# Reordering the first steps and the last steps of a top-k attention and highway kernel, and warming TensorE from the start

## The chip, the cores and the metric

The kernel runs on one core of a Trainium2 chip. The metric is the device time of the whole program in microseconds (us), taken as the median of several runs; lower is better. A profile of one execution goes with it. Its span, from the first to the last instruction, is a little shorter than the time of the same run.

Engine names as the profile writes them: PE is TensorE (matmuls; PEld is its weight load), DVE is VectorE, ACT is ScalarE, POOL is GpSimd, SP is SyncE, which here only issues transfers.

## The reference

Two things are computed, one after the other: attention in which every query keeps only its 32 largest scores, and a highway layer on the joined heads.

```python
# q, k, v: (8 batches, 8 heads, 576 rows, 64), float32
scores = (q @ k.T) / sqrt(64)
kth    = 32nd largest of each row
attn   = softmax(where(scores >= kth, scores, -1e9))
x      = (attn @ v), heads joined            # (4608, 512)
H = maximum(x @ w_h, 0)
T = 1 / (1 + exp(-(x @ w_t + b_t)))
out = T * H + (1 - T) * x                    # (4608, 512)
```

## The kernel before

The work is cut into 144 pairs. A pair is 128 query rows of two heads (or, for the 64 rows left over in each batch, of four heads at half height), and 18 pairs make a batch. The main loop is a pipeline over steps: step `n` evacuates and searches pair `n` while it multiplies pair `n + 1`, transposes pair `n - 4` and multiplies the values of pair `n - 5`. Two pairs, that is four rows of scores in each partition, are searched together as one quad. The names of the tiles are the ones in the profile:

- `kin`, `qin`, `krest`, `qrest`, `qc`: inputs as loaded. PE transposes them into a PSUM tile `kqps`, and a copy brings them to `kq`.
- `ps`: raw scores in PSUM (one buffer of four banks). ACT copies them with a ReLU to `z`.
- `hi`, `hh`, `h`: the row of 576 folded to 288, 144 and 72 by pairwise maxima on DVE. POOL makes the minima of the folds in the same tiles.
- `m`, `w`: lists of the largest values, from MAX8 and MATCH_REPLACE8 on DVE. Their end is the threshold.
- `pen`: ACT's penalty for what lies below the threshold. PE transposes `z` and adds the scaled penalty in PSUM (`zr`, `zt`), ACT takes the exponential into `et`, and PE multiplies it by the values `v` into `zr`, from which ACT copies `xs`.
- `x`, `xT`, `hps`, `tps`, `t`, `d`, `o`: the highway layer of one group of rows, in three parts "x" (transpose `x`), "h" and "t" (the two matmuls).

The opening and the loop, cut to what matters:

```python
def turn(self, pr, name, hp, bank=None, c0=0):       # transpose inputs on PE
    pool, tag = (self.ztps, "zt") if bank else (self.fps, "fp")
    ...
    nc.scalar.copy(dst, kqps[:, c0 * P : J * P])

def spin(n):
    for _ in range(n):
        ops.nc.tensor.transpose(warm[:, 0:P], ident[:], ident[:])

spin(12)
ops.turn(pr, "kin", 0, True)
ops.turn_first(pr, 0, 1)
ops.turn_rest(pr, 0, 1, ("krest",))
# ... loads
ops.scores(0, *pairs[0], preps[0])
ops.evac(0)
ops.turn_first(pr, 1, NHP)
ops.turn(pr, "kin", 1, True)
ops.turn_rest(pr, 1, NHP, ("krest",))

while step <= NPR:
    n = step
    if have(n):
        ops.tree(n)                                  # DVE: hi <- max of halves
        if n % 2:
            ops.minima(n // 2, ops.folds(n // 2, *pairs[n - 1], fill))
        if n + 2 < NHP:
            ops.turn(pr, "kin", n + 2, True)
        ...
    # ... masks of pair n - 4, values of pair n - 5
    if have(n + 1):
        ops.scores(n + 1, g, pi, preps[g.b])         # PE, needs ps free
        ops.evac(n + 1)                              # ACT: z <- relu(ps)
    # ... "x" and "h" of the highway layer
    if kind == "t":
        ops.ffn_t(fg)                                # PE tps, ACT t, t
    if n % 2:
        # ... rest of the lists of the quad before
        if n == 1:
            opening = ops.lists(0, *pairs[0])
            ops.run(opening, 2)                      # 4 MAX8, 4 MATCH_REPLACE8
    else:
        gens = opening if n == 2 else ops.lists(n - 2, *pairs[n - 2])
        # ...
    if nextg:
        ops.ffn_x(nextg)                             # joint group: PE xtps, ACT xT
    if have(n - 4):
        ops.trans(n - 4)                             # PE zr, zt; ACT et
    ...
```

`nextg` occurs four times: every second batch the two halves of 64 left-over rows form a joint group, which ends right behind another group. Its transposes take one of the two `zt` buffers that the transposes of `z` use as well.

`tree(n)` reads `ps` itself for `n >= 2`, so that the scores of pair `n + 1` can't be multiplied before `tree(n)` is done on DVE; for the first two pairs it reads `z` only.

The end of the program finishes the last two groups `gp` and `gl`, in whose order DVE, ACT and PE work as written:

```python
ops.ffn_e(gp)
ops.ffn_o(gp, *out_rows(gp))        # POOL: o <- d - x, then a transfer
...
ops.final_norm(gl, 3, 4)            # DVE: x of the last two heads
...                                 # PE transposes it, DVE: xT, PE: hps, t
judge_last(gl)                      # DVE: are the lists good enough?
ops.ffn_d(gl)
ops.final_t(gl, 3, 4)
judge()                             # PE: turn 128 verdicts, DVE: flag
ops.final_o(gl, out_rows(gl), (nc.sync, ops.nc.scalar))   # DVE: d, o, d, o; transfers
...
taken = nc.values_load(flag[0:1, 0:1], min_val=0, max_val=1)
with tc.If(taken > 0):              # an exact second pass, not taken here
```

Of the kernel before, what the change touches and what calls it, by code (L numbers as in the profile page):

```python
# [11 lines left out]
FP32 = mybir.dt.float32  # L12
# [7 lines left out]
J = 4  # L20
NZ = 3
NPEN = 3


class Pinned:
# [42 lines left out]
class Ops:  # L68
# [103 lines left out]
    def turn(self, pr, name, hp, bank=None, c0=0):  # L172


        nc, P = self.nc, self.P
        t = pr.pop((name, hp))
        pool, tag = (self.ztps, "zt") if bank else (self.fps, "fp")
        kqps = pool.tile([P, 512], FP32, tag=tag, name="kqps")
        for c in range(c0, J):
            nc.tensor.transpose(  # L180
                kqps[:, c * P : (c + 1) * P],
                t[:, c, :, :].rearrange("p h d -> p (h d)"),
                self.ident[:],
            )
        dst = pr["kq"][:, "kq".index(name[0]), hp, c0 * P : J * P]
        nc.scalar.copy(dst, kqps[:, c0 * P : J * P])

    def turn_rest(self, pr, h0, h1, names=("krest", "qrest")):

# [444 lines left out]
            if i1 == n_g:  # L634
                nc.scalar.activation(tp, tp, AF.Tanh)

    def final_o(self, g, dsts, queues):


        vec, P = self.nc.vector, self.P  # L640
        W = self.dm // 2
        n = P // len(dsts)
        o = self.fpool.tile([P, self.dm], FP32, tag="o", name="o")
        for j, tp in enumerate(g.tp):
            cs = slice(j * W, (j + 1) * W)
            vec.scalar_tensor_tensor(
                out=g.d[:, cs], in0=tp, scalar=1.0, in1=g.d[:, cs],
                op0=ALU.add, op1=ALU.mult,
            )
            vec.tensor_tensor(o[:, cs], g.d[:, cs], g.x[:, cs], ALU.subtract)  # L650
            for i, dst in enumerate(dsts):
                queues[j].dma_start(dst[:, cs], o[i * n : (i + 1) * n, cs])

    def ffn_bank(self, g, name, other=False):
        if g.last:
# [102 lines left out]
    def ffn_o(self, g, *dsts):  # L758
        ql = g.rows
        n = ql // len(dsts)  # L760
        if not self.exact and not g.last:
            for i, dst in enumerate(dsts):
                self.nc.gpsimd.dma_start(
                    dst, g.t[i * n : (i + 1) * n, :], accum_op=ALU.add
                )
            return
        o = self.fpool.tile([self.P, self.dm], FP32, tag="o", name="o")
        self.nc.gpsimd.tensor_tensor(
            o[0:ql, :], g.d[0:ql, :], g.x[0:ql, :], ALU.subtract
        )  # L770
        for i, dst in enumerate(dsts):
            self.nc.sync.dma_start(dst, o[i * n : (i + 1) * n, :])
# [3 lines left out]
def kernel(  # L776
# [25 lines left out]
    def const(shape, dt, name):  # L802
        return consts.tile(shape, dt, tag=name, name=name)

    ident = const([P, P], FP32, "ident")
    make_identity(nc, ident[:])
    nident = const([P, P], BF16, "nident")
# [34 lines left out]
    with ExitStack() as cm:  # L842
# [53 lines left out]
                ops.load_values(pr)  # L896

        for b in range(1, B):
            f = first[b] - 17
            for hp in range(NHP):  # L900
                at(f + 3 * hp, begin, b, hp)
                for i, name in enumerate(("kin", "qin")):
                    at(
                        f + 3 + 3 * hp + i,
                        lambda b, name, hp: ops.turn(preps[b], name, hp),
                        b, name, hp,
                    )
            at(f + 5, lambda b: ops.turn_rest(preps[b], 0, NHP), b)
            at(f + 8, lambda b: ops.values_rest(preps[b]), b)
            at(f + 11, lambda b: ops.values(preps[b], 0), b)  # L910
            at(f + 14, lambda b: ops.values(preps[b], 1), b)
# [11 lines left out]
        ops.load_first(pr, queue, 2, H)  # L923
        ops.load_rest(pr, "krest", queue, 2, H)
        ops.load(pr, "kin", 2, queue)
        warm = ops.fps.tile([P, 512], FP32, tag="fp", name="warm")

        def spin(n):
            for _ in range(n):
                ops.nc.tensor.transpose(warm[:, 0:P], ident[:], ident[:])  # L930

        spin(12)
        ops.turn(pr, "kin", 0, True)
        ops.turn_first(pr, 0, 1)
        ops.turn_rest(pr, 0, 1, ("krest",))
# [6 lines left out]
        ops.evac(0)  # L942
        ops.turn_first(pr, 1, NHP)
        ops.load_rest(pr, "qrest", queue, tag="qc")
        ops.turn(pr, "kin", 1, True)
        ops.turn_rest(pr, 1, NHP, ("krest",))
        ffn = []
        step = 0
# [32 lines left out]
# [3 lines that stand above are left out]
                ops.tree(n)  # L984
                if n % 2:
                    ops.minima(n // 2, ops.folds(n // 2, *pairs[n - 1], fill))
                    fill = []
                if n + 2 < NHP:
                    ops.turn(pr, "kin", n + 2, True)
                if NHP <= n + 1 < 2 * NHP:  # L990
                    ops.turn(pr, "qin", n + 1 - NHP, None, 1)
                if n == NHP:
                    ops.load(pr, "qin", 3, None, None, 1)
                if n == 2 * NHP:
                    ops.turn_rest(pr, 0, NHP, ("qrest",))
            if n == 5:
                load_weights()
            if have(n - 4):
                ops.mask(n - 4, *pairs[n - 4], tis=(0,))
            kind = fg = None  # L1000
            nextg = None
            if ffn and (ffn[0][0] != "x" or n % 2):
                kind, fg = ffn.pop(0)
                if kind == "t" and ffn and ffn[0][0] == "x":
                    nextg = ffn.pop(0)[1]
            if have(n - 5):
                values(n - 5)
            if have(n - 4):
                ops.mask(n - 4, *pairs[n - 4], tis=(1,))
            if have(n + 1):  # L1010
                g, pi = pairs[n + 1]
                ops.scores(n + 1, g, pi, preps[g.b])
                ops.evac(n + 1)
            if kind == "x":
                ops.ffn_x(fg)
            if kind == "h":
                ops.ffn_h(fg)
                ops.ffn_r(fg)
                ops.ffn_d(fg)
            if kind == "t":  # L1020
                ops.ffn_t(fg)
                if n < NPR - 1:
                    ops.ffn_e(fg)
                    ops.ffn_o(fg, *out_rows(fg))
            if n == 3:
                ops.values_rest(pr)
                ops.values(pr, 0)
            if n == 4:
                ops.values(pr, 1)
            ended = False  # L1030
            if have(n - 5):
                g, pi = pairs[n - 5]
                ended = pi == len(g.pairs) - 1 and (not g.rem or g.r0 > 0)
            if n % 2:
                gens = ops.lists_rest(n // 2 - 1, *pairs[n - 3]) if have(n - 3) else []
                late = gens[2:]
                gens = gens[0:2]
                if n == 1:
                    opening = ops.lists(0, *pairs[0])
                    ops.run(opening, 2)  # L1040
                ops.run(gens)
                ops.run(late, 2)
            else:
                ops.run(late)
                if n == 2:
                    gens = opening
                else:
                    gens = ops.lists(n - 2, *pairs[n - 2]) if have(n - 2) else []
                    ops.run(gens, 2)
                if ended:  # L1050
                    ops.norm(pairs[n - 5][0])
                ops.run(gens, 3)
                if have(n + 1):
                    gens, fill = gens[0:2], gens[2:4]
                ops.run(gens)
            if nextg:
                ops.ffn_x(nextg)
            if have(n - 4):
                ops.trans(n - 4)
            if ended and not pairs[n - 5][0].last:  # L1060
                ops.norm_heads(pairs[n - 5][0])
            for piece in pieces.pop(n, []):
                piece()
            if n % 2 == 0 and have(n - 3):
                g, pi = pairs[n - 3]
                if pi == len(g.pairs) - 1:
                    ops.settle(g)
            if ended:
                g = pairs[n - 5][0]
                ffn += [("x", g), ("h", g), ("t", g)]  # L1070
            step += 1
# [20 lines left out]
        ops.run(gens)  # L1092
        ops.mask(m + 1, *pairs[m + 1])
        ops.ffn_h(gp)
        ops.run(late)
        ops.settle(gl)
        ops.mask(m + 2, *pairs[m + 2])
# [1 line left out]
        ops.final_norm(gl, 0, 2)  # L1099
        ops.trans(m + 1)  # L1100
        ops.ffn_r(gp)
        ops.ffn_d(gp, ops.ffn_t(gp))
        judge_lists()
        judge_scales()
        part, ends = ops.parts(
# [12 lines left out]
        gl.ps = ops.fps.tile([P, 512], FP32, tag="fp", name="hps")  # L1118
        ops.final_norm(gl, 2, 3)
        ops.ffn_e(gp)  # L1120
        ops.ffn_o(gp, *out_rows(gp))
        values(m + 2)
        ops.final_h(gl, 0, 2)
        ops.final_turn(
            gl, 2, 3, ops.ztps.tile([P, 512], FP32, tag="zt", name="xtps")
        )
        ops.final_norm(gl, 3, 4)
        ops.final_t(gl, 0, 2)
        ops.final_turn(
            gl, 3, 4, ops.ztps.tile([P, 512], FP32, tag="zt", name="xtps")  # L1130
# [4 lines left out]
        ops.final_h(gl, 3, 4)  # L1135
        ops.ffn_d(gl)
        ops.final_t(gl, 3, 4)
        judge()
        ops.final_o(gl, out_rows(gl), (nc.sync, ops.nc.scalar))

    taken = nc.values_load(flag[0:1, 0:1], min_val=0, max_val=1)
    with tc.If(taken > 0):
# [72 lines left out]
```

## Time and profile before

| | |
|---|---|
| time, median of 3 runs | 838.0 us (837.43 to 838.75) |
| the profiled run | 837.23 us, span 835.4 us |
| DVE busy | 813.4 us, 97% of the span |
| ACT busy | 760.8 us, 91% |
| PE busy | 698.5 us, 84% |
| POOL busy | 711.5 us, 85% |
| share of DVE in the chain of work that ended last | 83% |
| transfers | 58.12 MB, 70 GB/s in the mean |

Busy time is the time in which an engine executes something; the rest of the span it waits. The chain of work that ended last is followed back from the last instruction: at each step either the instruction before it on the same engine, or, where the engine had been waiting, the one that released it. The timeline lists instructions in order of time: start, duration, engine, line, operation, result and operands, shapes, how many of them, and in square brackets how long the engine had been idle and what ended that. Nearly all operations carry line 35, a recording helper, so that they are told apart by their tiles. The clock of TensorE is given as the share of full speed that was granted; it is known from 7.4 us of the span on, and shown as 1.00 before that.

### The profile page before, as it was taken

The numbers are of one execution on the slowest core, as the hardware profiler recorded it, in microseconds if no ns is written. First come the engines' busy times: TensorE is split into PE (matmuls) and PEld (weight loads), VectorE is DVE, ScalarE is ACT, GpSimd is POOL, SyncE is SP. The second block draws the span as 40 slices with busy tenths as digits, with TensorE's granted clock in tenths as the row PEclk, the third lists the DMA queues.
The fourth block names the chain that finished last, engine by engine and source line by source line (L and its number), as shares of the span: only waits on it lengthen the run. The fifth ranks groups of instructions, "written<-read, shape, count | busy, mean of one in ns | idle before, by whom it ended". The sixth has DMA issues, their size and how long they took to land.

```text
span 835.4 us, 20051 instructions
## 1 busy us (share of the span) xinstructions
PE 698.5 (84%) x6520; PEld 488.4 (58%) x6566; DVE 813.4 (97%) x4169; ACT 760.8 (91%) x1522; POOL 711.5 (85%) x457
## 2 busy tenths in 40 slices
PE   6688888888888888788888898878888888878875
PEld 4466556565566556665556565656556665556554
DVE  4999999999999999999999999999999999999896
ACT  4799999899999999899999999989999999888894
POOL 6788888898889889878889988888888989887882
PEclk9999999999999999999999999999999999999898
DMA  8563523234254431333325242323413211111221
GB/s 191 135 110 71 115 39 67 57 69 96 39 100 86 78 89 32 72 70 66 88 52 98 64 112 41 64 58 67 111 40 67 50 31 34 40 39 27 38 39 43
DMA packets 105184, 58.12 MB, mean 70 GB/s; under 512 B 82288, under 2 KB 91888, under 8 KB 105072
## 3 DMA queue, kind: packets, MB, share of 16 engines
q1 hardware_dynamic: 93200, 37.47, 17.6%
q0 software_dynamic: 11056, 19.01, 15.6%
q8 instruction: 53, 0.87, 0.4%
q14 instruction: 59, 0.48, 0.2%
q10 hardware_dynamic: 816, 0.30, 0.1%
HBM read 30.67 MB, written 18.35 MB: 59 GB/s over the span
## 4 chain that ended last, share of the span: by engine, by line
DVE 83%; ACT 8%; PE 7%; issue 1%; POOL 1%; DVEq 0%; ACTq 0%; POOLq 0%
DVE w L35 46%; DVE m L35 18%; DVE hi L35 10%; DVE hh L35 5%; DVE h L35 3%; ACT pen L35 2%; PE zt L35 2%; PE ps L35 2%; ACT z L35 1%; ACT x L35 1%; ACT et L35 1%; ACT t L35 1%; PE hps L35 1%; PE zr L35 1%; DVE scales L35 0%
## 5 line engine op out<-in xcount | busy, mean ns | idle before, releaser
L35 PE MATMUL ps<-kq 64*128 64x64 f32 (+3 forms) x1280 | 206.7, 446 | 50.4 <-DVE hi L35 47.2
L35 ACT ACTIVATE pen<-z,m 128x576 bf16<-128x576 f32 x288 | 226.6, 788 | 1.1 <-DVE m L35 0.9
L35 PE MATMUL zt<-ident,z 128*128 128x128 f32 x1148 | 215.4, 281 | 6.1 <-ACT xT L35 6.1
L35 PE MATMUL zt<-nident,pen 128*128 128x128 bf16 x1148 | 205.9, 220 | 0.0
L35 ACT ACTIVATE z<-ps 128x1152 f32<-128x1152 f32 x144 | 162.8, 1131 | 46.8 <-PE ps L35 44.3
L35 POOL TENSOR_TENSOR hi<-z,hi 128x1152 int32<-128x1152 int32 x72 | 189.3, 2630 | 12.4 <-DVE m L35 6.9
L35 POOL TENSOR_TENSOR hi<-hi,z 128x1152 int32<-128x1152 int32 x72 | 190.3, 2643 | 5.6
L35 PEld LDWEIGHTS ps<-kq 64*128 64x128 f32 (+1 forms) x1280 | 104.9, 180 | 145.4 <-issue 81.7
L35 PEld LDWEIGHTS zt<-ident,z 128*128 128x128 f32 x1148 | 163.1, 142 | 21.3 <-ACT xT L35 7.0
L35 ACT ACTIVATE et<-zt 128x512 bf16<-128x512 f32 x287 | 162.5, 601 | 7.6 <-PE zt L35 3.8
L35 POOL TENSOR_TENSOR hh<-hi,hh 128x576 int32<-128x576 int32 x71 | 103.3, 1455 | 71.7 <-DVE w L35 71.7
L35 PEld LDWEIGHTS <-pen 128*128 128x128 bf16 x1440 | 152.4, 106 | 16.1 <-ACT pen L35 10.7
L35 DVE MAX8 m<-w 128x8 f32<-128x168 f32 x576 | 159.2, 316 | 0.0
L35 PE MATMUL zr<-v,et 128*128 128x65 bf16 (+1 forms) x1590 | 98.5, 196 | 46.1 <-ACT et L35 38.6
L35 PEld LDWEIGHTS <-et 128*128 128x128 bf16 (+1 forms) x1600 | 69.3, 101 | 84.4 <-ACT et L35 82.1
L35 DVE MAX8 w<-hi 128x8 f32<-128x288 f32 x288 | 115.8, 441 | 0.1
L35 DVE TENSOR_TENSOR hi<-ps,z 128x576 f32<-128x576 f32 x142 | 104.7, 738 | 4.3 <-ACT z L35 3.9
L35 POOL TENSOR_TENSOR hh<-hh,hi 128x576 int32<-128x576 int32 x71 | 100.3, 1412 | 5.6
L35 DVE MAX8 w<-hh 128x8 f32<-128x72 f32 x576 | 96.8, 219 | 0.0
L35 DVE MATCH_REPLACE8 w<-m,w 128x168 f32<-128x168 f32 x288 | 88.8, 314 | 0.0
L35 PE MATMUL zr<-ident,z 128*128 128x128 f32 x286 | 68.9, 294 | 9.2 <-ACT xs L35 9.2
L35 ACT ACTIVATE x<-xs,scales 128x64 f32<-128x64 f32 x272 | 68.2, 336 | 0.0
(96 smaller groups left out, 1152.3 us busy)
## 6 DMA issues: line engine op xcount, KB each, us to landing
x<-d POOLq DMA_DIRECT2D x34, 256.0 KB, 3.9
vin<-in_v_dram SPq DMA_DIRECT2D x8, 1024.0 KB, 5.5
kin<-in_k_dram SPq DMA_DIRECT2D x63, 128.0 KB, 3.3
out_dram<-d SPq DMA_DIRECT2D x30, 256.0 KB, 2.2
out_dram<-t POOLq DMA_DIRECT2D x30, 256.0 KB, 4.1
qin<-in_q_dram SPq DMA_DIRECT2D x56, 128.0 KB, 2.9
qrest<-in_q_dram SPq DMA_DIRECT2D x8, 128.0 KB, 3.8
vrest<-in_v_dram SPq DMA_DIRECT2D x8, 128.0 KB, 2.8
```

What stands on the lines that cost most here:

```text
L35: return self._tc.keep_in_program_order(fn(*args, **kw))
```

## The change

It moves work, and adds a little, in five places:

1. The first quad is searched whole in step 2: its first eight list operations no longer stand ahead of `tree(2)` on DVE.
2. TensorE is kept at work from the start. A tile of zeros, which DVE fills first of all, takes the place of the identity that POOL builds; 8 matmuls of 512 columns on it stand in front of the first transposes, and 9, 7 and 8 more behind the scores of steps 1, 2 and 3. They write to a PSUM tile that nobody reads.
3. In the opening, the copy of the transposed second `kin` goes to DVE, and the transposes of the third and fourth stand behind the scores of their step and not ahead of them. The loads and transposes for the second batch begin two steps later.
4. The transposes of a joint group's `x`, and with them ACT's copy `xT`, stand ahead of the "t" matmuls of the group before it, and no longer behind them and the lists.
5. At the end, the "t" matmuls of `gp` stand earlier, its last subtraction is done by DVE in place of POOL and stands behind the norm of the last heads, and the verdict and its flag are made behind the last output and not ahead of it.

```diff
+WARM = {1: 9, 2: 7, 3: 8}
...
     def turn(...):
-        nc.scalar.copy(dst, kqps[:, c0 * P : J * P])
+        copy = nc.vector.tensor_copy if bank == "V" else nc.scalar.copy
+        copy(dst, kqps[:, c0 * P : J * P])
...
     def final_o(self, g, dsts, queues, finish):
...
                 queues[j].dma_start(dst[:, cs], o[i * n : (i + 1) * n, cs])
+        finish()
...
     def ffn_o(...):
-        self.nc.gpsimd.tensor_tensor(
+        (self.nc.gpsimd if self.exact else self.nc.vector).tensor_tensor(
             o[0:ql, :], g.d[0:ql, :], g.x[0:ql, :], ALU.subtract
...
+    idle = const([P, 512], BF16, "idle")
+    nc.vector.memset(idle[:], 0.0)
...
-            f = first[b] - 17
+            f = first[b] - (17 if b > 1 else 15)
...
-        warm = ops.fps.tile([P, 512], FP32, tag="fp", name="warm")
         def spin(n):
+            if n:
+                warm = ops.ztps.tile([P, 512], FP32, tag="zt", name="warm")
             for _ in range(n):
-                ops.nc.tensor.transpose(warm[:, 0:P], ident[:], ident[:])
-        spin(12)
+                ops.nc.tensor.matmul(
+                    warm[:], idle[:, 0:P], idle[:], start=True, stop=True
+                )
+        spin(8)
...
-        ops.turn(pr, "kin", 1, True)
+        ops.turn(pr, "kin", 1, "V")
...
-                if n + 2 < NHP:
-                    ops.turn(pr, "kin", n + 2, True)
...
                 ops.scores(n + 1, g, pi, preps[g.b])
                 ops.evac(n + 1)
+                if n + 2 < NHP:
+                    ops.turn(pr, "kin", n + 2, True)
+            spin(WARM.get(n, 0))
             if kind == "x":
...
+            if nextg:
+                ops.ffn_x(nextg)
             if kind == "t":
                 ops.ffn_t(fg)
...
-                if n == 1:
-                    opening = ops.lists(0, *pairs[0])
-                    ops.run(opening, 2)
...
-                if n == 2:
-                    gens = opening
-                else:
-                    gens = ops.lists(n - 2, *pairs[n - 2]) if have(n - 2) else []
-                    ops.run(gens, 2)
+                gens = ops.lists(n - 2, *pairs[n - 2]) if have(n - 2) else []
+                ops.run(gens, 2)
...
-            if nextg:
-                ops.ffn_x(nextg)
...
         ops.ffn_h(gp)
+        h = ops.ffn_t(gp)
...
-        ops.ffn_d(gp, ops.ffn_t(gp))
+        ops.ffn_d(gp, h)
...
-        ops.ffn_o(gp, *out_rows(gp))
...
         ops.final_norm(gl, 3, 4)
+        ops.ffn_o(gp, *out_rows(gp))
...
-        judge()
-        ops.final_o(gl, out_rows(gl), (nc.sync, ops.nc.scalar))
+        ops.final_o(gl, out_rows(gl), (nc.sync, ops.nc.scalar), judge)
```

## The prediction

> **What bounds the kernel now.** I read the page's busy shares and its chain of work first: DVE is busy 813.4 of 835.4 us, and 83% of the chain that ended last is DVE.
>
> ```profile
> PE 698.5 (84%) x6520; PEld 488.4 (58%) x6566; DVE 813.4 (97%) x4169; ACT 760.8 (91%) x1522; POOL 711.5 (85%) x457
> ...
> DVE 83%; ACT 8%; PE 7%; issue 1%; POOL 1%; DVEq 0%; ACTq 0%; POOLq 0%
> ```
>
> So whatever the change does, it can only win time in which DVE waits: 835.4 - 813.4 = 22.0 us, or work that it takes from DVE (none; it adds three instructions). The next view is therefore the waits of DVE alone, and then the timeline around each.
>
> ```profile
> DVE kq L35 <- PE kqps L35: 8.2, 2, 5.6
> DVE hi L35 <- ACT z L35: 6.3, 4, 2.3
> DVE xT L35 <- PE xtps L35: 0.8, 2, 0.5
> DVE w L35 <- POOL room L35: 0.4, 1, 0.4
> ```
>
> They lie in three places. The opening: no work but two copies before 9.19 us, then a wait to 12.29 and one to 21.11, 12.2 us in all. The joint groups: 0.1 us each at 243, 443 and 644, and 2.5 us behind the fourth. The end: about 1.4 us of small waits, and 4.9 us from DVE's last result to the end. Between 22 and 226 us, and in all the long stretches between, DVE does not wait; nothing can be won there.
>
> The timeline of DVE in the opening, of PE there, of PE, ACT and DVE behind the fourth joint group, and of DVE and POOL at the end:
>
> ```profile
> 12.29 0.76 DVE L35 TENSOR_TENSOR hi<-z 128x576 f32<-128x576 f32 x1 [2.34 <-ACT z L35]
> ...
> 18.77 0.90 DVE L35 MAX8 w<-hh 128x8 f32<-128x72 f32 x6
> 21.11 0.76 DVE L35 TENSOR_TENSOR hi<-ps,z 128x576 f32<-128x576 f32 x1 [1.45 <-ACT z L35]
> ```
>
> ```profile
> 17.56 2.35 PE L35 MATMUL ps<-kq 64*128 64x512 f32 x8 [3.96 <-DVE hi L35]
> ...
> 22.02 1.30 PE L35 MATMUL ps<-kq 64*128 64x512 f32 x8 [1.28 <-DVE w L35]
> ```
>
> ```profile
> 774.74 0.33 PE L35 MATMUL zt<-ident,z 128*128 128x128 f32 x1 [1.73 <-ACT xT L35]
> ...
> 776.82 2.40 PE L35 MATMUL ps<-kq 64*128 64x512 f32 x8
> ```
>
> ```profile
> 779.26 1.13 ACT L35 ACTIVATE z<-ps 128x1152 f32<-128x1152 f32 x1 [1.40 <-PE ps L35]
> ```
>
> ```profile
> 780.42 0.76 DVE L35 TENSOR_TENSOR hi<-ps,z 128x576 f32<-128x576 f32 x1 [1.99 <-ACT z L35]
> ```
>
> ```profile
> 824.01 0.29 DVE L35 TENSOR_TENSOR x<-xs,scales 128x128 f32<-128x128 f32 x1
> ...
> 825.01 1.39 DVE L35 TENSOR_TENSOR x<-xs,scales 128x128 f32<-128x128 f32 x1
> ...
> 828.72 0.14 DVE L35 CAST flag<-flag_f 1x1 int32<-1x1 f32 x1
> ...
> 830.02 0.42 DVE L35 TENSOR_TENSOR o<-d,x 128x256 f32<-128x256 f32 x1
> ```
>
> ```profile
> 824.98 1.26 POOL L35 TENSOR_TENSOR o<-d,x 128x512 f32<-128x512 f32 x1 [4.34 <-DVE scales L35]
> ```
>
> To be seen: the same eight score matmuls take 1.30 us at full clock and 2.35 to 2.40 after TensorE had stood still; behind the fourth joint group the chain is ACT xT, PE zt, PE ps at half clock, ACT z, DVE hi; and at the end one and the same DVE operation takes 0.29 us, and 1.39 where POOL's o runs beside it.
>
> [...]
>
> **The change, part by part.**
>
> *First chain.* The first kin has landed at 4.09 us (from the transfers' landing times), and the 12 warm transposes hold PE until 4.19, so its transposes start at 4.22. The new tile of zeros is a short DVE fill that I put at 0.7 to 1.0 us, so warming starts about 0.5 us before today's 1.58. But eight 512-column matmuls at half clock take about 0.43 us each (the four "t" matmuls of the trace take 1.03 us at full clock, 0.21 each once they are pipelined), 3.4 us, and hold PE until about 4.45: the chain starts 0.2 us later. In return the clock rises, in the mean, 0.5 us earlier, which is worth half of that. [...]
>
> *Copies of the opening.* [...] The third kin is out of PE's way, so scores(1) start at 9.7 in place of 9.78. But its copy now stands behind z(1), from 12.1 to 12.65, and scores(2) need it: 12.7 in place of 12.30. They are done at 14.0, z(2) at 15.2, and DVE wants it at 15.4. It just fits: 0.1 us.
>
> *First quad.* tree(2) moves from 16.75 to 15.4, as the 4 MAX8 and 4 MATCH_REPLACE8 (15.40 to 16.75) now follow it. ps is free at 16.16. The 9 warm matmuls, 9 x 0.215 = 1.9 us, begin at 14.55 and end near 16.5; scores(3) run at full clock from 16.5 to 17.8, z(3) to 18.9. DVE's list work from tree(2) to tree(3) is 1.35 + 1.33 + 0.90 = 3.6 us less overlaps, so it comes to tree(3) at 19.65 and doesn't wait. Gain 21.11 - 19.65 = 1.46. Part of it is given back: POOL's two minima of the first quad (15.64 to 20.95) do not move, since they start when the folds end, and the two-input fold hh behind tree(3) now meets them (20.45 against 20.87), so it is held 0.4 us. Net 1.05 us. The later start of the second batch's loads takes work from a stretch in which DVE doesn't wait: 0.
>
> *Joint groups.* xT comes behind z and ahead of two activations of 0.58 and 0.63 us, so it ends 1.15 us earlier (773.54 for 774.69), and PE waits 0.5 us and not 1.73. ACT loses its gap of 0.33 us, comes to the next z at 777.5, and the scores, if the clock holds, end at 777.8. DVE gets z at 779.0 where it was ready at 778.44: it waits 0.56 in place of 1.99, and the later 0.50 and 0.11 go as well: 2.0 us. The other three give up 0.1 each. [...] I take 1.8 us.
>
> *End.* o costs DVE about 0.69 us (512 of 576 columns of a 0.76 us operation), but frees x of its lock: x ends at 825.30 for 826.39, o at 825.95, xT at 826.24 for 827.17. The d, o, d, o behind it then end at 829.2 for 830.45, also because flag and cast (0.41) stand behind them: 1.3 us sooner for the last transfer. But the flag is made at 829.55 for 828.86, 0.7 us later, and each engine loads it and branches on it. Before, SP branches at 830.2, 1.35 us after the flag because a transfer was in its way, and its first event behind the branch comes at 833.14, 0.03 us after the transfer issued by SP landed (833.11). So either landing (then the end gains 1.3) or the time behind the branch, 2.9 us on SP and 3.1 on DVE, sets the end; with the branch at flag + 1.0 = 830.55 the end would lose 0.3. I take +0.1.
>
> Sum: 0 + 0 + 1.05 + 1.8 + 0.1 = 3.0 us, so 838.0 - 3.0 = 835.0 us.
>
> **Rivals.** [...] (b) *The end gains in full*, because landing and not the branch sets it: 833.8. (c) *The joint groups give nothing*, as another wait takes the place of xT: ACT is at 91% and in these steps has no slack, so that z comes late whatever PE does: 836.8. Against it: ACT does wait for PE there, 0.33 and 1.40 us. (d) *DVE's new work at the front or at the end meets POOL*: the fill at 0.7 us lies in POOL's fills, but reads nothing.
>
> **Range and chances.** The parts have about these uncertainties: first chain 0.6, quad 0.5, joint groups 0.8, end 0.8, and 0.4 for the median of before, whose three runs differ by 1.3; their root of squares is 1.4. With 1.25 times that, 833.2 to 836.6. 2% is 16.8 us; there are only 22 us of waits, and 8 of them are before the first scores can exist. So within 2% is nearly certain: 0.98, with 0.01 on each side.
>
> **What would show it.** DVE's busy time about 815 us, and its waits down to some 16 us. tree(3) starting near 19.7 us without a wait before it, with hh held behind POOL; scores(3) at 1.30 us; PE's wait for xT near 0.5 us at all four joint groups, and DVE's wait behind the fourth below 0.8. At the end, x of the last heads at 0.29 us, the last o near 1.3 us sooner against the neighbouring work, and the branch of SP later. I am wrong in the opening if the first scores start later than 6.3 us and the clock rises no sooner; in the middle if DVE waits at places where it does not now; at the end if the last landing moves and the end follows it, or if it moves and the end stays by more than 0.5 us.

## The result, and the profile after

The changed kernel takes 835.29 us (median of 4 runs, 835.09 to 835.49), beside 838.38 us for the kernel before in the same series: the ratio is 0.996, with a 95% interval of 0.994 to 0.9979. A second series gave 834.78 us and 0.9969 (0.9958 to 0.998). So it is 2 to 3 us faster, 0.3 to 0.4%.

The page of the changed kernel, its busy shares and the shares of its chain of work:

```profile
PE 700.4 (84%) x6539; PEld 486.3 (58%) x6586; DVE 814.9 (98%) x4172; ACT 761.0 (91%) x1521; POOL 711.9 (85%) x456
...
DVE 92%; PE 2%; ACT 2%; POOL 2%; issue 1%; DVEq 0%; POOLq 0%
```

DVE has 1.5 us more to do (814.9 for 813.4) and still ends sooner: its share of the chain rose from 83% to 92%. The waits of DVE alone, in us in total, number of times and longest:

```profile
DVE kq L36 <- PE kqps L36: 7.1, 2, 4.8
DVE hi L36 <- ACT z L36: 2.3, 2, 2.0
DVE idle L809 <- PEq L1201: 0.9, 1, 0.9
```

The wait of `hi` for `z` fell from 6.3 us in four places to 2.3 in two, and the one of `xT` is no longer among the longest. The timeline of DVE in the opening, then of PE there:

```profile
9.64 0.75 DVE L36 TENSOR_TENSOR hi<-z 128x576 f32<-128x576 f32 x1
12.37 0.76 DVE L36 TENSOR_TENSOR hi<-z 128x576 f32<-128x576 f32 x1 [1.98 <-ACT z L36]
...
15.49 0.75 DVE L36 TENSOR_TENSOR hi<-ps,z 128x576 f32<-128x576 f32 x1
...
19.66 0.75 DVE L36 TENSOR_TENSOR hi<-ps,z 128x576 f32<-128x576 f32 x1
...
20.46 1.23 DVE L36 TENSOR_TENSOR hh<-hi 128x576 f32<-128x576 f32 x1
```

```profile
1.19 3.60 PE L36 MATMUL warm<-idle 128*128 128x512 bf16 x8 [1.19 <-DVE idle L809]
4.58 1.06 PE L36 MATMUL kqps<-ident,kin 128*128 128x128 f32 x4
```

```profile
6.33 1.72 PE L36 MATMUL ps<-kq 64*128 64x512 f32 x8 [0.18 <-ACT kq L36]
...
14.58 2.11 PE L36 MATMUL warm<-idle 128*128 128x512 bf16 x8
16.62 1.30 PE L36 MATMUL ps<-kq 64*128 64x512 f32 x8
```

The trees are the four `hi` lines. tree(0) starts 0.45 us later than before, tree(3) 1.45 sooner and without a wait, and `hh` behind it takes 1.23 us for 0.74, beside GpSimd's minimum that ends at 21.07 us: at tree(4) the lead is 0.97 us. The scores of pair 3 run at full clock (1.30 us, and a granted clock of 1.00 from 17 to 21 us, where the kernel before has 2.35 us and a granted 0.50 from 17.7 to 21.0). The fourth joint group, PE and then DVE:

```profile
773.22 0.33 PE L36 MATMUL zt<-ident,z 128*128 128x128 f32 x1 [0.56 <-ACT xT L36]
```

```profile
778.39 0.76 DVE L36 TENSOR_TENSOR hi<-ps,z 128x576 f32<-128x576 f32 x1 [0.33 <-ACT z L36]
```

DVE's wait behind it is 0.33 us in place of 1.99 (the granted clock is 1.00 from 775 to 783 us; the kernel before has 0.50 from 775.4 to 782.2), and the lead over the kernel before (how much sooner the same tree starts) grows from 0.38 us at tree 138 to 2.82 at tree 141. The end, on DVE:

```profile
822.14 0.29 DVE L36 TENSOR_TENSOR x<-xs,scales 128x128 f32<-128x128 f32 x1
822.35 0.69 DVE L36 TENSOR_TENSOR o<-d,x 128x512 f32<-128x512 f32 x1
...
825.13 0.43 DVE L36 TENSOR_TENSOR o<-d,x 128x256 f32<-128x256 f32 x1
...
825.92 0.42 DVE L36 TENSOR_TENSOR o<-d,x 128x256 f32<-128x256 f32 x1
...
826.57 0.14 DVE L36 CAST flag<-flag_f 1x1 int32<-1x1 f32 x1
```

`x` of the last heads is free (0.29 for 1.39). The last `o` ends at 826.35 us, 4.10 sooner than before, but the span ends only 1.67 us sooner, at 833.7. Behind the last `o` lie 7.36 us where 4.93 lay before: 2.4 us of what was gained ahead of it are gone there. The flag is ready at 826.71, 2.15 us sooner. The last transfer (ACT's) lands at 828.30 us, 5.41 us ahead of the end; in the kernel before it lands at 833.40, 1.98 ahead of it.

### The profile page after: what moved, and what is told of

Its sections match the earlier page's. It is cut to its first block, busy times and chain, and to the rows that moved or that the text cites. A ratio compares the mean times of both kernels' runs of the same rounds, so it can differ in the third digit from the quotient of the medians.

```text
span 833.7 us, 20096 instructions
## 1 busy us (share of the span) xinstructions
PE 700.4 (84%) x6539; PEld 486.3 (58%) x6586; DVE 814.9 (98%) x4172; ACT 761.0 (91%) x1521; POOL 711.9 (85%) x456
## 4 chain that ended last, share of the span: by engine, by line
DVE 92%; PE 2%; ACT 2%; POOL 2%; issue 1%; DVEq 0%; POOLq 0%
DVE w L36 51%; DVE m L36 20%; DVE hi L36 11%; DVE hh L36 6%; DVE h L36 3%; POOL hi L36 1%; POOL hh L36 1%; PE ps L36 1%; ACT z L36 1%; DVE scales L36 0%; ACT x L36 0%; PE warm L36 0%; ACT pen L36 0%; DVE d L36 0%; DVE ok L36 0%
## 5 line engine op out<-in xcount | busy, mean ns | idle before, releaser
L36 PE MATMUL ps<-kq 64*128 64x64 f32 (+3 forms) x1280 | 203.8, 441 | 49.2 <-DVE hi L36 45.9
```

The costliest lines, as they stand in the source:

```text
L36: return self._tc.keep_in_program_order(fn(*args, **kw))
```

## Experiments

Each run is compared with the kernel before on the same chip, in the same series; two rows of different series are compared through their gains alone. The gain is worked out as (1 - ratio) times the median of before (837.3 us in the first series, 837.15 in the second, 837.93 in the third), with its interval in the same way.

| run | what differs from the changed kernel | median us | gain over before, us |
|---|---|---|---|
| c_after | nothing | 834.78 | 2.6 (1.7 to 3.5) |
| u_joint | joint transposes at their old place | 836.36 | 1.3 (0.7 to 1.8) |
| u_end | the whole end as before | 834.85 | 2.4 (1.6 to 3.3) |
| h_judge | the flag ahead of the last `o` | 833.13 | 4.1 (3.0 to 5.3) |
| u_warm | no zero tile, old warming | 835.68 | 1.2 (0.3 to 1.9) |
| u_quad | first quad split as before | 835.11 | 1.9 (1.0 to 2.8) |
| u_wq | both | 836.5 | 0.5 (-0.2 to 1.2) |
| best7 | h_judge with 7 warm matmuls in front | 833.18 | 3.3 (2.3 to 4.5) |
| c_before | it is the kernel before | 838.0 | -0.4 (-1.4 to 0.6) |
| u_copy | opening's copies and transposes as before | 836.22 | 1.6 (0.6 to 2.5) |
| h_pool | h_judge with `o` of `gp` on GpSimd | 834.48 | 2.9 (1.9 to 4.0) |
| x_noif | no branch on the flag | 832.12 | 5.1 (3.5 to 6.6) |

Differences below a microsecond between two rows are inside their intervals, unless the traces below show the event itself.

**c_after**, the changed kernel once more, without an edit.

> The changed kernel again, beside the kernel before on the same chip: the reference for the parts below. Theory: its gain of about 3 us is made up of +1.0 us in the opening, +2.6 us at the joint groups, and -0.9 us from the last pair to the end, with 0.5 us lost to a slightly slower pace of every engine in that one execution. Expected: span 833.3 to 833.8, lead over before about 1 us at the fifth pair. If the slower pace belongs to the change (contention of POOL and DVE), it comes again: the steps between two joint groups take 0.01 us more than before's each; if it was the execution or the chip, it is gone or as large elsewhere.

Measured: 834.78 us, 2.6 us of gain, and a trace whose lead is 1.49 us at tree(4), 1.31 at tree 138 and 3.95 at tree 141. The span, 832.8 us, is shorter than expected, and from tree(4) to tree 138 only 0.18 us are lost, where the first profile lost 0.59: most of that slower pace belonged to the one execution. The opening differs from that of the first profile by more than half a microsecond, with not one instruction changed: the eight scores of pair 0 start at 5.80 us and take 1.30. The same PE lines as above, here:

```profile
1.19 3.50 PE L36 MATMUL warm<-idle 128*128 128x512 bf16 x8 [1.19 <-DVE idle L809]
4.52 0.60 PE L36 MATMUL kqps<-ident,kin 128*128 128x128 f32 x4
...
5.80 1.30 PE L36 MATMUL ps<-kq 64*128 64x512 f32 x8 [0.36 <-ACT kq L36]
```

The first four transposes take 0.60 us and not 1.06. The clock is up before the first real work. The first profile of the changed kernel had been an unlucky one.

**u_warm, u_quad, u_wq and c_before**: warming and the first quad, undone alone and together, and the kernel before in a second profile.

```diff
 u_warm
-WARM = {1: 9, 2: 7, 3: 8}
+WARM = {}
-    idle = const([P, 512], BF16, "idle")
-    nc.vector.memset(idle[:], 0.0)
-                ops.nc.tensor.matmul(warm[:], idle[:, 0:P], idle[:], start=True, stop=True)
+                ops.nc.tensor.transpose(warm[:, 0:P], ident[:], ident[:])
-        spin(8)
+        spin(12)
 u_quad
+                if n == 1:
+                    opening = ops.lists(0, *pairs[0])
+                    ops.run(opening, 2)
-                gens = ops.lists(n - 2, *pairs[n - 2]) if have(n - 2) else []
-                ops.run(gens, 2)
+                if n == 2:
+                    gens = opening
+                else:
+                    gens = ops.lists(n - 2, *pairs[n - 2]) if have(n - 2) else []
+                    ops.run(gens, 2)
```

> The changed kernel with the warming undone: no zero tile, the 12 identity transposes in front again, and no warm matmuls behind the first quads; the whole first quad and all else stay. Theory of my prediction (the order does it): tree(2) at 15.5 us ends the wait for ps at about 16.3, TensorE's gap before scores(3) is about 2 us, too short for the clock to fall, scores(3) take 1.30 us and tree(3) starts within 0.3 us of 19.66; the time is within 0.3 us of the changed kernel's. Rival (the warm matmuls hold the clock): scores(3) take 2.3 us at half clock, tree(3) waits and starts near 20.6, of which hh's hold behind the minima takes back 0.4: 0.5 to 1.0 us slower than the changed kernel. Third (the front of the program): with the 12 transposes the clock rises some 0.2 us later and the first scores start some 0.3 us sooner; tree(0) within 0.5 us of 9.64.

> The changed kernel with the first quad split again as before (half of the opening lists ahead of tree(2)), the zero tile and the warm matmuls kept. If the order alone made the gain: tree(2) at 16.8, tree(3) at about 21, 1.0 us slower than the changed kernel. If the clock made it: scores(3) start near 17.6 but take 1.30 us, tree(3) starts near 20.1, where hh no longer meets the minima, and the lead at tree(4) is within 0.1 us of the changed kernel's: the time within 0.2 us of it.

> The changed kernel with both undone, the warming and the whole first quad. Both theories of the opening: scores(3) at half clock, tree(3) near 21, and 1.0 us slower than the changed kernel (1.0 to 1.5). If this is no slower than the changed kernel, the opening gave nothing, and the gain of 3 us lies in the joint groups and elsewhere.

> The kernel before once more, for a second profile of its opening and its joint groups. If the identity transposes leave the clock's rise to chance: the first scores take anything between 1.97 and 2.40 us, at no run 1.30, and tree(0) starts between 9.2 and 10.9 us (9.19 in the first profile, 10.9 in the two profiles with the identity transposes put back). [...] Time as before, 837.2 within 0.5.

Measured, starts in us from the profiles:

| profile | scores(0): start, took | tree(0) | tree(1) | tree(3), wait | scores(3) took | `hh` took | tree(4) |
|---|---|---|---|---|---|---|---|
| before | 6.00, 1.97 | 9.19 | 12.29 | 21.11, 1.45 | 2.35 | 0.74 | 26.92 |
| c_before | 6.21, 2.40 | 9.96 | 13.52 | 22.41, 1.50 | 2.40 | 0.74 | 28.21 |
| u_wq | 6.09, 2.40 | 10.82 | 13.55 | 21.41, 0.48 | 1.30 | 0.74 | 27.22 |
| u_warm | 6.18, 2.40 | 10.91 | 13.64 | 20.94, none | 1.30 | 1.20 | 27.20 |
| u_quad | 5.64, 1.30 | 9.12 | 11.85 | 19.71, 0.48 | 1.30 | 0.74 | 25.52 |
| c_after | 5.80, 1.30 | 9.12 | 11.85 | 19.15, none | 1.30 | 1.22 | 25.43 |
| after | 6.33, 1.72 | 9.64 | 12.37 | 19.66, none | 1.30 | 1.23 | 25.95 |

The kernel before has its first scores on PE at half clock, all or in part (2.40 and 1.97 us, where full clock takes 1.30), and so has u_wq (2.40), from which the lines of PE and then of DVE follow:

```profile
4.22 1.09 PE L35 MATMUL kqps<-ident,kin 128*128 128x128 f32 x4
...
6.00 1.97 PE L35 MATMUL ps<-kq 64*128 64x512 f32 x8 [0.18 <-ACT kq L35]
```

```profile
1.58 2.82 PE L36 MATMUL warm<-ident 128*128 128x128 f32 x12 [1.58 <-POOL ident masks.py:199]
4.32 1.09 PE L36 MATMUL kqps<-ident,kin 128*128 128x128 f32 x4
```

```profile
18.02 0.75 DVE L36 TENSOR_TENSOR hi<-ps,z 128x576 f32<-128x576 f32 x1
...
21.41 0.76 DVE L36 TENSOR_TENSOR hi<-ps,z 128x576 f32<-128x576 f32 x1 [0.48 <-ACT z L36]
...
22.23 0.74 DVE L36 TENSOR_TENSOR hh<-hi 128x576 f32<-128x576 f32 x1
```

With the identity transposes in front, the scores of pair 0 take 1.97 to 2.40 us in all four profiles, and tree(0) starts at 9.19 to 10.91. With the zero tile they take 1.30 us in nine of ten profiles (the first profile of the changed kernel is the tenth), and tree(0) starts at 8.70 to 9.64. In time, undoing the warming costs 1.4 us (2.6 against 1.2 of gain): u_warm's expectation of 0.3 us missed, and the expectation that its tree(0) would stay within 0.5 us of 9.64 missed by 0.8. The 1.4 us need not be the clock alone: in u_warm DVE's copy of the second `kin` (0.69 us) stands ahead of tree(0), which comes later (10.91) than in both profiles of the kernel before (9.19 and 9.96). The expectation's theory for scores(3) held: they stay at full clock with no warm matmul behind the first quad. TensorE stands still for 1.64 us ahead of them there, and for 3.96 us in the kernel before. u_wq's expectation missed: scores(3) run at full clock (1.30 us), and yet the gain is 2.1 us smaller than that of the changed kernel, not 1.0 to 1.5.

The second reading concerns the quad. At full clock the old order makes DVE wait 0.48 us before tree(3), as in u_quad:

```profile
19.71 0.76 DVE L36 TENSOR_TENSOR hi<-ps,z 128x576 f32<-128x576 f32 x1 [0.48 <-ACT z L36]
```

The new one makes it wait not at all; but then `hh` is held 0.46 to 0.49 us by GpSimd's minima, and from tree(0) to tree(4) u_quad needs 16.40 us and c_after 16.31. So the order itself is worth 0.09 us in the trace. u_quad's second expectation held there. The 1.45 us of before consist of 0.48 of order and about 1 us of half clock, and u_wq, with the old order and no warming, doesn't have that half clock. c_before does (2.40 us). What keeps u_wq from it isn't shown: it may be chance, but u_wq also has the third and fourth `kin` transposed behind the scores of their step, and TensorE stands still for 2.98 us ahead of scores(3), against 3.96 us in both profiles of the kernel before. No run tells the two apart. c_before's expectation of its first scores held (2.40 us), and its time came out at 838.0 us, where 836.7 to 837.7 had been expected. In time u_quad lost 0.7 us against c_after, and the intervals of the two overlap.

**u_copy**: the copies and transposes of the opening undone.

```diff
-            f = first[b] - (17 if b > 1 else 15)
+            f = first[b] - 17
-        ops.turn(pr, "kin", 1, "V")
+        ops.turn(pr, "kin", 1, True)
+                if n + 2 < NHP:                     # ahead of the scores again
+                    ops.turn(pr, "kin", n + 2, True)
```

> The changed kernel with the copies of the opening undone: the second kin is copied by ScalarE again, the third and fourth are turned ahead of the scores, and the second batch begins at its old step. My prediction: 0.1 us of cost in all, so the time is within 0.2 us of the changed kernel's. Seen: scores(1) start within 0.2 us after their old distance from tree(0) (0.59 us), scores(2) 0.5 us sooner. Rival (the second batch's later start matters, or DVE's copy delays tree(1)): 0.5 us or more to either side.

Measured: a gain of 1.6 us for 2.6 with the copies, so that this group of edits (the later start of the second batch with them, which no run undoes alone) is worth about 1.0 us and costs nothing; the intervals overlap, but the trace shows 0.83 us of it as early as tree(4) (26.26 us for 25.43 in c_after). The rival had the size and not the cause: what the lines below show is neither DVE's copy nor the second batch. The expectation on scores(1) missed by a wide margin: they start 1.47 us behind tree(0), not 0.6; scores(2) start at 12.72 us, 0.1 sooner than in the first profile of the changed kernel and not 0.5. PE of u_copy, then of c_after:

```profile
8.57 0.40 PE L36 MATMUL kqps<-ident,krest 64*128 64x64 f32 x3
9.63 0.63 PE L36 MATMUL kqps<-ident,kin 128*128 128x128 f32 x4 [0.66 <-DMA kin<-in_k_dram]
10.19 1.30 PE L36 MATMUL ps<-kq 64*128 64x512 f32 x8
```

```profile
9.35 1.30 PE L36 MATMUL ps<-kq 64*128 64x512 f32 x8 [0.57 <-DVE kq L36]
```

The transposes of the third `kin` stand ahead of the scores in PE's queue and wait 0.66 us for its transfer; with their own 0.56 us they delay scores that don't need them. From tree(0) to tree(1) u_copy needs 3.98 us. All profiles with the new copies need 2.72 to 2.73, and the two of the kernel before 3.10 and 3.56. In those the wait for the transfer could not be seen: with the half-clock scores ahead of them, PE came to these transposes at 9.22 and 10.43 us, and the third `kin` had landed at 9.08 and 9.30. u_copy's PE was there at 8.97, and the landing came at 9.50.

**u_joint**: the joint transposes back behind the lists.

```diff
-            if nextg:
-                ops.ffn_x(nextg)
             if kind == "t":
...
+            if nextg:
+                ops.ffn_x(nextg)
             if have(n - 4):
```

> The change without the part on the joint groups (their transposes and xT stand behind the gate and the lists again). Theory 'xT holds PE': DVE waits 0.1 us again at the first three joint groups and 0.8 to 2.5 us behind the fourth, by where the half-clock window falls: span 834.4 to 836.5, so 1 to 3 us over the changed kernel. Rival 'ACT has no slack there, the order doesn't matter': within 0.3 us of the changed kernel.

Measured: 1.3 us of gain for 2.6, so these moves are worth 1.3 us. Its fourth joint group on PE, then DVE behind it:

```profile
773.34 0.33 PE L36 MATMUL zt<-ident,z 128*128 128x128 f32 x1 [1.73 <-ACT xT L36]
...
775.43 2.40 PE L36 MATMUL ps<-kq 64*128 64x512 f32 x8
```

```profile
779.03 0.76 DVE L36 TENSOR_TENSOR hi<-ps,z 128x576 f32<-128x576 f32 x1 [2.00 <-ACT z L36]
...
785.50 0.76 DVE L36 TENSOR_TENSOR hi<-ps,z 128x576 f32<-128x576 f32 x1 [0.49 <-ACT z L36]
```

The old wait for `xT` (1.73 us for 0.56), the half clock behind it and DVE's 2.00 and 0.49 us are all back. Against c_after the trace loses 2.65 us between trees 138 and 141; the median of 20 runs loses 1.3 us, and those runs lie in two clusters, 834.3 to 834.9 and 836 to 837.3. That fits a half clock which comes in some executions and not in others. The profiles agree: at the fourth joint group the scores run at half clock in all three with the old order (before, c_before, u_joint) and in one of the eleven with the new one. That one is u_copy:

```profile
773.44 0.33 PE L36 MATMUL zt<-ident,z 128*128 128x128 f32 x1 [0.56 <-ACT xT L36]
...
776.12 2.40 PE L36 MATMUL ps<-kq 64*128 64x512 f32 x8
```

PE's wait for `xT` is the short one there, and DVE waits 1.44 us behind it all the same. So the new order makes the half clock rarer at this place and doesn't rule it out.

**u_end, h_judge, h_pool and x_noif**: the end.

```diff
 u_end (and "t" of gp and ffn_o of gp at their old places)
-        (self.nc.gpsimd if self.exact else self.nc.vector).tensor_tensor(
+        self.nc.gpsimd.tensor_tensor(
 u_end, h_judge, h_pool
-        ops.final_o(gl, out_rows(gl), (nc.sync, ops.nc.scalar), judge)
+        judge()
+        ops.final_o(gl, out_rows(gl), (nc.sync, ops.nc.scalar), lambda: None)
 h_pool: the flag as in h_judge, and GpSimd's o at its NEW place
 x_noif
-    taken = nc.values_load(flag[0:1, 0:1], min_val=0, max_val=1)
-    with tc.If(taken > 0):
-        ...                          # the exact second pass
```

x_noif leaves out the load of the flag, the branch and the second pass behind it. The flag is still computed.

> The change with the whole end as it was (o of the group before the last on POOL, t matmuls late, verdict ahead of the last output). Theory 'the end is set by the flag, the branch behind it and what follows the branch': x of the last heads is locked again (1.39 us), the last output comes 1.4 us later, yet the flag 0.5 us sooner, and the span gets 0.9 us shorter, about 832.6. Rival 'the end is set by the landing of the last transfer': the span gets 1.3 us longer, about 834.9.

> The change, with the verdict and its flag ahead of the last output again, but o still on DVE. Theory 'flag and branch set the end': the flag comes near 825.0 in place of 826.7, SP branches about 1.1 us sooner, and no longer together with the other engines; the span gets 1.3 to 2.0 us shorter, 831.6 to 832.4. Rival 'landing sets the end': the last output comes 0.45 us later and the span gets 0.4 us longer.

> The changed kernel with the flag ahead of the last o, and o of the group before it on GpSimd at its new place. If the new place alone frees x from GpSimd: both x stay at 0.29 us, DVE has 0.69 us less ahead of the last xT, and the end comes 0.5 us sooner than with o on VectorE (833.1), about 832.6. Rival (GpSimd's 1.26 us of o lock DVE's operations there as they locked x): xT or d beside it take 0.6 to 1.1 us longer, and the time is 833.1 or above.

> The changed kernel without the load of the flag, the branch on it and the exact second computation behind it (left out); the judge and its flag are still computed. If the flag and the branch set the end, and not the last landing: the end comes 1.9 us (landing) and some 2.2 us of closing work behind the last o at about 826.3, near 830.5 of span in place of 832.8 to 833.7, 2.5 to 3 us below the changed kernel's time. Rival (the landing and the closing waits set it): within 0.7 us of the changed kernel.

Measured, in us of the span:

| profile | flag ready | last `o` ends | SP's branch | first event behind it | end | flag to end | last `o` to end | last landing to end |
|---|---|---|---|---|---|---|---|---|
| before | 828.86 | 830.45 | 830.22 | 833.14 | 835.38 | 6.52 | 4.93 | 1.98 |
| after | 826.71 | 826.35 | 827.63 | 831.47 | 833.71 | 7.00 | 7.36 | 5.41 |
| c_after | 826.22 | 825.86 | 827.14 | 830.54 | 832.78 | 6.56 | 6.92 | 4.97 |
| u_end | 826.08 | 827.67 | 827.44 | 832.03 | 834.92 | 8.84 | 7.25 | 1.98 |
| h_judge | 825.01 | 826.59 | 826.37 | 828.88 | 831.36 | 6.35 | 4.77 | 1.98 |
| h_pool | 825.61 | 827.20 | 826.97 | 829.86 | 832.26 | 6.65 | 5.07 | 1.98 |
| x_noif | 826.08 | 825.72 | none | none | 829.66 | 3.58 | 3.95 | 1.99 |

The end follows the flag: in eleven of the thirteen profiles with a branch it comes 6.35 to 7.11 us behind it, whichever of the two orders a kernel has, while the distance from the last `o` runs from 4.77 to 7.40 in the same eleven (the other two, u_joint and u_end, have 7.38 and 8.84 from the flag).

But SP also waits for the landings behind its branch, and the last column shows when that counts. In the seven profiles with the flag last the end comes 4.88 to 5.80 us behind the last landing and 2.22 to 2.24 us behind SP's first event behind the branch: the branch alone sets it. In the six with the flag ahead of the last `o` (four of the table, c_before and best7) it comes 1.98 us behind the last landing, as in x_noif (1.99), so there the landing comes last. It costs 0.1 to 0.9 us more than the branch alone would (2.32 to 3.14 us from SP's first event, for 2.24), and in the first profile of the kernel before nothing: there the two come together within 0.01 us. In these six the last two transfers are under way while the engines branch, and take 2.8 to 5.6 us from issue to landing; with the flag last they take 1.9.

Without the branch the end comes 3.95 us behind the last `o`, and x_noif gains 2.5 us more than c_after. So with the flag last a cost of about 3 us stands behind it and overlaps with nothing. h_judge puts the last two `o` and their transfers beside it, and about 0.8 us of it are left (4.77 from the last `o` to the end, for 3.95). DVE at the end of h_judge:

```profile
824.87 0.14 DVE L36 CAST flag<-flag_f 1x1 int32<-1x1 f32 x1
...
826.17 0.42 DVE L36 TENSOR_TENSOR o<-d,x 128x256 f32<-128x256 f32 x1
```

h_judge keeps all else of the changed kernel and gains 4.1 us in place of 2.6. Its five runs (832.69 to 834.14 us) lie below all seven of c_after (834.2 to 835.84). It has the largest gain of the versions that compute everything, with best7's interval (below) overlapping its own. What the 3 us consist of is shown in part: the queues of instructions start to move packets 0.3 to 0.7 us behind SP's branch (before, after, u_end, h_judge), SP's first event comes 2.5 to 4.6 us behind its branch, and 3 us of the end vanish with the branch (6.92 us from the last `o` in c_after, 3.95 in x_noif). That SP waits for these packets, and that they slow the transfers beside them, isn't shown.

u_end differs from h_judge in that GpSimd makes `o` of `gp` at the old place, and in the place of the "t" matmuls. It gains 1.7 us less than h_judge, and the two intervals overlap by 0.3 us. So the new end consists, by time, of two parts of about 1.6 us with opposite signs: the free `x` wins it, the late flag gives it back. In the traces the free `x` is worth 1.1 us (from the start of the last `x` to the end of the last `o` 4.36 us in h_judge and 5.44 in u_end). The span of u_end in the table is no measure: its profile is of the slowest of its nine runs (836.68 us, median 834.85), in which the transfers took longest. By the median, neither size that had been expected of u_end came true. h_pool missed. POOL and DVE of h_pool:

```profile
821.74 1.26 POOL L36 TENSOR_TENSOR o<-d,x 128x512 f32<-128x512 f32 x1
```

```profile
821.76 1.39 DVE L36 TENSOR_TENSOR x<-xs,scales 128x128 f32<-128x128 f32 x1
```

GpSimd starts `o` as soon as its input is there, 0.02 us ahead of the last `x`, and so meets it at the new place as well. From `x` to the last `o` pass 5.44 us again, as in u_end, so neither the new place nor the earlier "t" matmuls count here. It is the engine that frees `x`, and not the order: 0.29 us in h_judge with `o` on DVE, 1.39 here with `o` on GpSimd at the same place.

**best7**: h_judge with one warm matmul fewer in front.

```diff
-        spin(8)
+        spin(7)
```

> The changed kernel with the flag ahead of the last o again (o of the group before it stays on VectorE at its new place), and 7 warm matmuls in front for 8. If the eighth warm matmul holds TensorE past the landing of the first kin (4.26 us, its transposes start at 4.58), then the transposes start at about 4.3, tree(0) 0.3 us sooner, and the time is some 0.3 us below that of the version with the flag ahead alone (833.1), about 832.8. [...]

Measured: 833.18 us, no gain, and the expectation missed. The transposes do start at 4.21 us for 4.58, and the first scores 0.22 us sooner, but tree(0) starts at 9.23 for 8.89. At full clock PE waits next for a transfer:

```profile
7.60 0.52 PE L36 MATMUL kqps<-ident,qc 128*128 128x128 f32 x3 [0.60 <-DMA qc<-in_q_dram]
```

In h_judge the same transposes start at 7.26 us without a wait. From there the chain goes over DVE's two copies, which now stand ahead of tree(0). `qc` lands at 7.46 us in best7 and at 7.12 in h_judge. When it lands decides, and no longer when the first transposes start.

## Why the prediction was right or wrong

The time came out at 835.29 us for 835.0 predicted, a gain of 3.1 for 3.0 in that pair and 2.6 in the second. The sum is right, two of its five terms are not, and the reason of a third isn't. That the sum came out within 0.4 us is in part luck: by time the first chain and the copies gave more than predicted, the quad and the joint groups less.

*First chain, predicted 0, was wrong.* In the pair of profiles it looks right: scores at 6.33 us, later than my 6.3, tree(0) 0.45 later, and the clock up only some 0.2 us sooner, as I estimate from the time of those scores (1.72 us for 1.97, between the 1.30 of full and the 2.40 of half clock). That profile was the unlucky one of ten. The step that failed is "the clock rises, in the mean, 0.5 us earlier, which is worth half of that", which I had assumed and no run shows: with the zero tile the clock is up before the first scores (1.30 us) in nine of ten profiles, and with the identity (1.97 to 2.40 us) in none of four, and the warming is worth 1.4 us by time (u_warm). I counted both fillers as the same kind of busy time. They differ in more than kind: the twelve transposes also start 0.4 us later (1.58 us for 1.19) and last 0.8 us less (2.82 for 3.60), and no run tells kind from length.

*Copies of the opening, predicted 0.1 us of cost, were wrong.* The start of scores(1) that I gave, 9.7, and of scores(2), 12.7, came out as 9.87 and 12.86. The 9.7 rests on a time of DVE's copy that no run shows; the copy took 0.69 us (u_wq). What failed is "9.7 in place of 9.78", the old order's time, taken from a trace at half clock. At full clock the old order waits for the landing of a `kin` that isn't needed yet (0.66 us), and the copies and the later transposes are worth 1.0 us (u_copy).

*First quad, predicted 1.05 us net, was right in size and wrong in its reason.* tree(3) without a wait at 19.66 us for 19.65, `hh` held 0.49 us for 0.4, and from tree(1) to tree(4) 13.58 us for 14.63: exactly 1.05. But the order is worth only 0.09 of it (u_quad); the rest is the half clock on scores(3), which the old order has in both profiles of the kernel before (2.35 and 2.40 us) and not in u_wq and u_quad (1.30). So most of that gain is the clock's and not the order's, and my own step did not tell the two apart. What kept the clock up in u_wq, chance or TensorE's shorter standstill (2.98 us for 3.96), stays open.

*Joint groups, predicted 1.8 us, were right.* PE's wait is 0.56 us for 0.5, DVE's 0.33 for 0.56, the 0.50 and 0.11 are gone, and the trace wins 2.44 us for 2.3 (2.0 and three times 0.1). u_joint gives 1.3 us by time, so that the 0.5 us by which I took less than the 2.3 were needed and a little too few. No run shows in which executions the half clock comes; of the profiles, all three with the old order have it at the fourth joint group, and one of the eleven with the new. Rival (c) falls.

*End, predicted +0.1 us, was right by a cancellation, and its parts were named.* Measured from `x` on, the last `o` came 1.2 us sooner for 1.3, and the flag 0.7 later for 0.7. I left open whether the landing or the branch sets the end and took the middle. In the changed kernel it is the flag and the branch (h_judge, x_noif): its last landing is 5.41 us ahead of the end. In the kernel before the two come together within 0.01 us, so that its trace alone couldn't tell. Rival (b) falls: 2.4 us of the lead at the last `o` were given back. By time the whole new end is worth 0.2 us (u_end). Missed was the price behind it: an order which keeps the free `x` and not the late flag brings 1.5 us more.

Of the signs I had listed, DVE's busy time held (815), its waits did not reach 16 us (833.7 - 814.9 = 18.8), and that difference lies behind the last `o`. GpSimd's fill did not meet the new DVE work (rival d): the zero tile took 0.27 us.

The parts don't add: undoing them one by one loses 1.4, 1.0, 0.7, 1.3 and 0.2 us, 4.6 in all, where the whole gains 2.6 to 3.1. With such intervals (about 1 us each) that is no contradiction. The copies in particular pay only behind a front that is fast: behind a slow one DVE's second copy delays tree(0) (u_warm).

## What to carry to other kernels

A trace taken at half clock can hide waits that a full clock uncovers, as here the one for the third `kin` (0.66 us). So before pricing an order in an opening, look at whether the same matmuls appear at two durations (here the eight of the scores, 1.30 and 2.40 us), and take a second profile. Where a program ends in a branch on a computed flag, make the flag as early as possible and put the last outputs and their transfers behind it; here that order was worth 1.5 us of 835. And when the engine that frees an operation and its place in the order change together, test them apart: here only the engine counted.

## What the runs showed of the hardware that was not expected

- Seven or eight matmuls of 512 columns on zeros brought the clock up by the first transposes (4.2 to 4.6 us) in eight of ten profiles and before the first scores in nine, and 12 identity transposes brought it up before the first scores in none of four. The first four transposes took 0.60 us behind the zeros in c_after and 1.06 in the first profile of the changed kernel, and the first scores 1.30 us behind zeros in the nine and 1.97 to 2.40 behind the identity. Zeros were work enough for the clock here.
- The last two transfers, of 128 KB each, land 1.9 us after their issue in the changed kernel and in x_noif. In the kernel before, where they are under way while the engines branch, they take 3.3 and 2.9 us, and in u_end 5.6 and 5.2, with packets of the instruction queues beside them (8 between 828 and 836 us in the kernel before, from 0.3 us behind SP's branch on). The time from the last landing to the end is 1.98 us in all six profiles with the flag ahead of the last `o`.
- From the branch to SP's first event behind it pass 2.5 to 4.6 us, and two profiles of the same code differ by 0.4 us there (3.84 and 3.40).
- Between the opening and the fourth joint group the lead of the changed kernel's first profile fell from 0.97 to about 0.4 us with no new wait. c_after and h_judge have the same code there and differ by 0.4 us over 130 pairs, so that no reading of a few tenths across the whole program was made from a single pair of traces.
